# GpSimd's position tables ahead of its first two loads, in an attention and expert kernel whose loads all go through one queue

## The chip, the core and the metric

The kernel runs on one core of a Trainium2 chip. The core has five engines that run side by side, each with its own list of instructions: TensorE (PE, with its weight loads shown apart as PEld), VectorE (DVE), ScalarE (ACT), GpSimd (POOL) and SyncE (SP). Sixteen DMA engines move data between the device memory and the core. SP and POOL issue the transfers of this kernel: what SP issues is listed as hardware_dynamic (queue q1), what POOL issues as software_dynamic (queue q0). The metric is the device time of one execution in microseconds; lower is better.

## What is computed

Attention over 4 batches, 8 heads, 768 positions and 64 values a head, with a mask for each head, followed by a mixture of 8 experts with 4 slots each:

```python
scores = scale * np.matmul(q, k.transpose(0, 1, 3, 2))
pos = np.arange(S)
rel = pos[:, None] - pos[None, :]
causal = rel >= 0
stream_keep = causal & (is_sink | in_win)          # the first 4 keys, or the last 64
mask = np.where(retr, full_mask, stream_mask)      # by head
a = softmax(np.where(mask, scores, -1e9))
x = np.matmul(a, v)  # then reshaped to (3072, 512)
logits = x @ phi                                   # 32 slots
d = softmax of logits over the tokens
slot_input = d.T @ x
h = np.maximum(slot_input[e] @ w1[e], 0.0); slot_out[e] = h @ w2[e]   # e = 0..7
out = softmax of logits over the slots @ slot_out
```

The inputs are float32: q, k and v of 6.3 MB each and w1 and w2 of 16.8 MB each. POOL's loads convert to bfloat16 on the way.

## The kernel before

The kernel first makes a list of operations (`pl.op`), each with the engines that can run it, a priority, what it depends on and a function `emit` that writes its instructions. A planner (`Plan.run`, line 69) puts them in order by its own estimates of time; the functions are then called in that order (lines 1178 to 1185), and the order in which they are called is the order of the instructions on each engine. Within one `emit`, the instructions follow each other as they are written.

All loads but three are issued by POOL through the helper `dma` (line 343), which appends to a chain: each issue depends on the one before (`fifo[0]`), and from the ninth on also on the landing of the load eight places ahead (line 345). So POOL's issues have a fixed order: the first halves of q, k and v of batch 0 (`load_part`, line 361), their second halves, half of the first expert's w1, then tiles of the other batches with weights between them, and at the end the last w2 in halves (lines 976 to 979), which are put into memory that the attention has set free.

The three other loads are SP's (`sp_front`, line 480), issued without any wait: the other half of the first expert's w1 in float32 (1 MB, `w0f`), the head flags (`ri`) and phi (`phf`).

`tables` (line 412) is what the change moves: six small instructions on POOL.

```python
def tables(o):
    nc.gpsimd.iota(jrow, ...)          # 128x128, column numbers
    nc.gpsimd.iota(pc[:, 0:1], ...)    # 128x1, partition numbers
    nc.gpsimd.iota(tq, ...)            # 1x256
    nc.gpsimd.iota(krow, ...)          # 1x128
    nc.gpsimd.memset(unit, 1.0)        # 1x256
    nc.gpsimd.iota(pc_i[:, 0:1], ...)  # 128x1, integers
```

From the first two VectorE makes the identity (`head_const`, line 422), which ScalarE reorders for the first transposes (`ident_u`, line 500); from the others TensorE and VectorE make the distances between positions for the masks (`emit_td`, `key_pos`, lines 429 to 442) and the slots' tables (line 465). All of these operations depend on the operation `tables` (`o_tab`, line 488).

On POOL the order at the start is: issue of q's first half, issue of k's first half, `tables`, issue of v's first half, two memsets (`ones`), issues of the second halves. TensorE transposes the first half of q when it has landed and the reordered identity is there (`transposes`, line 599); until then it runs matmuls on zeros (`fill`, line 425). Phi is cast, transposed twice and spread in between (lines 548 to 555).

After the attention come the expert layers: each expert's w1 product and w2 product as its weights land (lines 1008 to 1084), then the product that makes the output (`out_tile`, line 1125) and the stores (`store`, line 1146), most of them from SP.

Of the kernel before, what the change touches and what calls it, by code (L numbers as in the profile page):

```python
# [226 lines left out]
def kernel(  # L227
# [81 lines left out]
    def tr_bf(s, n):  # L309
        return trb[s].bitcast(BF16)[:, 0:n]  # L310
# [10 lines left out]
    pl = Plan({"S8": 11, "QT": 2, "KT": 2, "VT": 1, "VB": 2, "VF": 3, "PT": 2, "PTX": 2, "XB": 2,  # L321
               "XT": 1, "SC": 2, "TR": 2, "PV": 1, "BK": 8})
# [6 lines left out]
    def on(eng, occ, late=0.18):  # L329
        return {eng: (occ, occ + late)}  # L330

    def copy(o, dst, src):
        if o.eng == "ACT":
            nc.scalar.copy(dst, src)  # L334
        else:
            nc.vector.tensor_copy(dst, src)  # L336
# [4 lines left out]
    fifo, chain = [None], []  # L341

    def dma(name, nbytes, buf, dst, src, deps=()):
        if len(chain) >= 8:
            deps = list(deps) + [chain[-8]]
        iss = pl.op("issue " + name, on("POOL", 0.645, 1.4), -100, deps=list(deps) + [fifo[0]],
                    acq=[buf] if buf else [], lead=1.3, emit=lambda o: nc.gpsimd.dma_start(dst(), src))  # L347
        fifo[0] = iss
        took = nbytes / (395000.0 if nbytes == 1 << 20 and name != "w0" else 423000.0)
        chain.append(pl.op("land " + name, {"DMA": (took, took + 1.85 + 0.05 * len(chain))}, -100, deps=[iss] + chain[-1:], lead=5.2))  # L350
        return chain[-1]

    def raw_view(buf, p0, p1):
        return slots[buf.slot][p0:p1, 0:8 * KB].rearrange("p (i x) -> p i x", i=2)

    def raw_src(x, b, n0, n1):
        a = srcs[x][b].rearrange("(i n) (t s) d -> n t i (s d)", i=2, s=32)[n0:n1]
        return a.rearrange("n t i x -> (n t) i x")


    def load_part(x, b, part=None):
        if part is None:
            raws[x, b] = buf = Buf("S8")
            lands[x, b] = dma(f"{x}{b}", 96 * 2 * 8192, buf, lambda: raw_view(buf, 0, 96), raw_src(x, b, 0, 4))
        else:
            if part == 0:
                raws[x, b] = Buf("S8")
            buf = raws[x, b]
            src = srcs[x][b].rearrange("(i n) (y s) d -> n y i (s d)", i=2, s=16)[2 * part:2 * part + 2]
            lands[x, b, part] = dma(f"{x}{b}.{part}", 96 * 2 * 4096, buf if part == 0 else None,  # L370
                                    lambda: half_view(buf, part), src.rearrange("n y i e -> (n y) i e"))

    def half_view(buf, part):
        return slots[buf.slot][0:96, 2048 * part:2048 * (part + 1)].rearrange("p (i x) -> p i x", i=2)
# [6 lines left out]
    def w_mem(i):  # L381

        m = late_mem[i]() if i in late_mem else slots[wbuf[i].slot][:, :]
        return m.rearrange("p (h x) -> p h x", h=2)[:, :, 0:4 * KB]
# [27 lines left out]
    def tables(o):  # L412
        nc.gpsimd.iota(jrow, [[1, 128]], base=0, channel_multiplier=0, allow_small_or_imprecise_dtypes=True)
        nc.gpsimd.iota(pc[:, 0:1], [[0, 1]], base=0, channel_multiplier=1, allow_small_or_imprecise_dtypes=True)
        nc.gpsimd.iota(tq, [[128, 2], [1, 32], [32, 4]], base=0, channel_multiplier=0,
                       allow_small_or_imprecise_dtypes=True)
        nc.gpsimd.iota(krow, [[-1, 32], [-32, 4]], base=0, channel_multiplier=0,
                       allow_small_or_imprecise_dtypes=True)
        nc.gpsimd.memset(unit, 1.0)
        nc.gpsimd.iota(pc_i[:, 0:1], [[0, 1]], base=0, channel_multiplier=1)  # L420
# [33 lines left out]
    def head_flags(o, n):  # L454
        cp = nc.scalar.copy if o.eng == "ACT" else nc.gpsimd.tensor_copy
        for a, j0, j1 in ((1, 1, 4), (0, 0, 1)):
            cp(fmx[:, n, :, j0:j1, :].rearrange("p i j d -> p i (j d)"),
               thr[:, a, n::4].rearrange("p (i o) -> p i o", o=1).to_broadcast([P, 2, 66 * (j1 - j0)]))
# [24 lines left out]
        nc.sync.dma_start(phf, moe_phi.rearrange("(p a) s -> p (a s)", a=4))  # L483

    load_part("q", 0, 0)
    load_part("k", 0, 0)
    o_sp = pl.op("front", on("SP", 2.0, 4.8), -100, emit=sp_front)
    fifo[0] = o_tab = pl.op("tables", on("POOL", 1.65, 0.0), -100, deps=[fifo[0]], emit=tables)
    load_part("v", 0, 0)
    def pone(o):  # L490
        for b_ in vbs:
# [33 lines left out]
    for n in range(4):  # L525
        o_fm[n] = pl.op(f"fm{n}", on("ACT", 0.65) if n == 0 else on("POOL", 0.9), -8 if n == 0 else T * n - 3.5,
                        deps=[o_fl], emit=lambda o, n=n: head_flags(o, n))
# [15 lines left out]
    def phi_t2(o):  # L543
        for n in range(4):
# [8 lines left out]
                  emit=lambda o: nc.vector.tensor_copy(  # L553
                      phi4, tr_bf(pb2.slot, 4 * NS).rearrange("p (n r s) -> p n r s", n=4, r=1).to_broadcast(
                          [P, 4, 4, NS])))
# [3 lines left out]
    def load_tile(ti):  # L559

        tbuf[ti], tland[ti], p0 = Buf("S8"), [], 0
        for x, b, x0, x1 in TILES[ti]:
# [8 lines left out]
                  emit=lambda o, x=x: nc.gpsimd.tensor_copy(w_mem(0)[:, 0, KB * x:KB * (x + 1)],  # L571
                                                            w0f[:, KB * x:KB * (x + 1)])) for x in range(4)]
# [82 lines left out]
    def evs(x, b, n):  # L655
        return ev[x, 0, n // 2] if b == 0 else [e for x0, x1, e in ev[x, b] if x0 < 6 * n + 6 and x1 > 6 * n]
# [15 lines left out]
    def mask_emit(b, n, g):  # L672
        def f(o):
            pT = pTs[PTb[b, n].slot]
            mh = msk[:, n::4, :]
            if g < 2:
                pT = pT[:, :, 1024 * g:1024 * (g + 1)].rearrange("p i (a c) -> p i a c", a=2)[:, :, :, 0:256]
                mh = mh[:, :, 256 * g:256 * g + 512].rearrange("p i (a c) -> p i a c", a=2)
            else:
                pT, mh = pT[:, :, 2048:2304], mh[:, :, 256:512]  # L680
            nc.vector.tensor_tensor(pT, pT, mh, op=ALU.mult)  # L681
        return f
# [6 lines left out]
    for b in range(B):  # L689
        for n in range(4):  # L690
# [5 lines left out]
            def emit_v2(o, n=n, tr=tr):  # L696
                t = tr_bf(tr.slot, 768)
                for j in range(6):
# [3 lines left out]
                      emit=emit_v2, mode="full", mm=6)  # L702
# [9 lines left out]
            def emit_vf(o, b=b, n=n, p=p):  # L712
# [4 lines left out]
                           emit=emit_vf)  # L717

            PTb[b, n] = Buf("PT")
            for kk, g in enumerate(range(5)):  # L720
# [19 lines left out]
                for m, gs in enumerate(MGROUPS):  # L740
                    if gs[-1] == g:
                        o_m = pl.op(f"MK.{p}.{m}", on("DVE", [0.605, 0.605, 0.335][m]), key + 0.3,
                                    deps=[expo[p, x] for x in gs] + [o_hm[n]], emit=mask_emit(b, n, m))
# [3 lines left out]
        for ns in ([(0, 1), (2, 3)] if b == 0 else [(0, 1, 2, 3)]):  # L747
            sc = Buf("SC")

            def emit_lx(o, b=b, sc=sc, ns=ns):  # L750
# [4 lines left out]
                      deps=list(dict.fromkeys(e for n in ns for x in "qk" for e in evs(x, b, n))),  # L755
# [10 lines left out]
            def emit_mx(o, b=b, ns=ns):  # L766
# [5 lines left out]
                      emit=emit_mx)  # L772
# [5 lines left out]
    for b in range(B):  # L778
        for n in range(4):
# [9 lines left out]
            for i in iorder:  # L789
                deps, need = [v2e[p], vfo[p]] + [o_z][p:], set()  # L790
# [7 lines left out]
                def emit_pv(o, b=b, n=n, p=p, i=i, pv_at=pv_at):  # L798
                    pT = pTs[PTb[b, n].slot]
                    vb = vbs[VBb[b].slot]  # L800
                    for h in range(2):
                        bk, c = pv_at(h, i)
                        for j in range(i + 1):
# [3 lines left out]
                            else:  # L807
# [5 lines left out]
                             deps=list(dict.fromkeys(deps)) + ([last] if last else []),  # L813
# [8 lines left out]
            for i0, i1 in halves:  # L822
                part = f"{p}" if i1 - i0 == 6 else f"{p}.{i0}"

                def emit_nm(o, i0=i0, i1=i1, b=b, n=n, p=p):
# [3 lines left out]
                    else:  # L829
# [8 lines left out]
                                 deps=[pvo[i1 - 1], XBb[b].op], acq=[XBb[b]] if n == 0 else [], rel=[PVb[p]],  # L838
                                 emit=emit_nm)
# [25 lines left out]
        if b < B - 1:  # L865
# [19 lines left out]
            def emit_tt(o, te=te):  # L885
                for i in range(6):
# [5 lines left out]
                           emit=lambda o, te=te: copy(o, elg.rearrange("p i s -> p (i s)"), tr_bf(te.slot, 6 * NS)))  # L892
# [8 lines left out]
        else:  # L901
# [3 lines left out]
            for i0 in (0, 3):  # L905
                a = pl.op(f"LG.{b}" if i0 else f"LGb.{b}", pe(25, 3), kb - 6.0, deps=[a, xhalf[i0]], rel=[XTb[b]],
                          emit=lambda o, lg=lg, f=emit_lg, i0=i0: f(o, lg, ns=(3,), i0=i0, i1=i0 + 3), mode="full", mm=3)
# [82 lines left out]
    def emit_si(o):  # L990
        t = trb[si.slot][:, 0:4 * NS].rearrange("p (a s) -> p a s", a=4)
        sv = slot_sc.rearrange("p (di do) -> p do di", do=4)
        for do in range(4):
# [4 lines left out]
                  emit=lambda o: nc.vector.tensor_copy(siT.rearrange("p a s -> p (a s)"), trb[si.slot][:, 0:4 * NS]))  # L998
# [110 lines left out]
    for c in range(2):  # L1109
        def emit_so(o, c=c):  # L1110
# [3 lines left out]
            else:  # L1114
# [3 lines left out]
                          emit=emit_so))  # L1118
# [103 lines left out]
```

## Time and profile before

| | us |
|---|---|
| median of 3 runs | 147.88 |
| lowest and highest | 147.87, 148.34 |
| the profiled execution | 147.56 |
| its span, first to last instruction | 145.8 |

The mean granted clock of TensorE over the span is 0.944 of the full one. How to read the rows that follow: in the timeline and the chain of waits the first number is the start in microseconds from the first instruction, the second the time taken, then engine, line and operation, what it writes and what it reads; in square brackets stands how long the engine sat idle before it and what ended the wait. SPq and POOLq are the two engines' own sequencers. A DMA instruction of POOL is shown while the descriptors are made, not while the data move. Landing is counted from the issue. In the table of DMA queues a row gives packets, megabytes written and the time of the packets as a share of sixteen engines; the share can exceed 100%, since packets of one engine overlap.

### The profile page before, as it was taken

The numbers are of one execution on the slowest core, as the hardware profiler recorded it, in microseconds if no ns is written. First come the engines' busy times: TensorE is split into PE (matmuls) and PEld (weight loads), VectorE is DVE, ScalarE is ACT, GpSimd is POOL, SyncE is SP. The second block draws the span as 40 slices with busy tenths as digits, with TensorE's granted clock in tenths as the row PEclk, the third lists the DMA queues.
The fourth block names the chain that finished last, engine by engine and source line by source line (L and its number), as shares of the span: only waits on it lengthen the run. The fifth ranks groups of instructions, "written<-read, shape, count | busy, mean of one in ns | idle before, by whom it ended". The sixth has DMA issues, their size and how long they took to land.

```text
span 145.8 us, 4941 instructions
## 1 busy us (share of the span) xinstructions
PE 124.6 (85%) x2134; PEld 82.3 (56%) x2134; DVE 110.8 (76%) x254; ACT 107.9 (74%) x147; POOL 40.5 (28%) x73
## 2 busy tenths in 40 slices
PE   6959989999999999999989999999959899869100
PEld 4437566676776758776548766666737355444000
DVE  1796399999999999999799899999983312449700
ACT  3152799999999988999998999999971461549300
POOL 6988631310311470100170011405380000110000
PEclk9985699999999999999999999999995999999965
DMA  5999999999999999999999999999999999999995
GB/s 135 277 208 211 215 215 214 212 216 214 215 214 214 216 215 214 216 214 211 215 214 215 214 216 219 212 217 215 217 210 215 211 194 197 185 321 362 407 420 247
DMA packets 14648, 33.40 MB, mean 229 GB/s; under 512 B 867, under 2 KB 7651, under 8 KB 14115
## 3 DMA queue, kind: packets, MB, share of 16 engines
q0 software_dynamic: 11184, 26.22, 92.9%
q1 hardware_dynamic: 3442, 6.88, 12.7%
q8 instruction: 16, 0.26, 0.6%
q14 instruction: 6, 0.04, 0.1%
HBM read 52.49 MB, written 6.29 MB: 403 GB/s over the span
## 4 chain that ended last, share of the span: by engine, by line
PE 28%; DVE 25%; DMA 18%; ACT 15%; issue 6%; POOL 1%; SPq 0%; DVEq 0%; ACTq 0%; POOLq 0%
DMA qk<-in_moe_w_dram 15%; ACT pt L735 11%; PE sc L665 6%; DVE pt L681 5%; PE pv L809 5%; DVE xv L833 5%; DMA phf<-in_moe_phi_dram 4%; DVE qk L336 3%; PE tr L613 3%; PE tr L639 3%; PE bk L1130 3%; PE tr L872 2%; DVE slot L1140 2%; DVE vf L714 2%; PE tr L845 2%
## 5 line engine op out<-in xcount | busy, mean ns | idle before, releaser
L735 ACT ACTIVATE pt<-sc 128x1024 bf16<-128x1024 f32 x80 | 77.0, 1049 | 3.0 <-PE sc L665 2.8
L665 PE MATMUL sc<-qk 64*128 64x512 bf16 (+3 forms) x256 | 31.3, 311 | 1.2 <-ACT pt L735 0.8
L681 DVE TENSOR_TENSOR pt<-pt,msk 128x1024 bf16<-128x1024 bf16 (+1 forms) x48 | 29.0, 609 | 2.0 <-ACT pt L735 1.8
L809 PEld LDWEIGHTS <-pt 128*128 128x128 bf16 x640 | 23.7, 98 | 6.2 <-issue 5.2
L809 PE MATMUL pv<-vx,pt 128*128 128x65 bf16 x320 | 25.9, 194 | 0.3 <-DVE xv L833 0.2
L809 PE MATMUL pv<-vf,pt 128*128 128x65 bf16 x320 | 21.6, 196 | 0.9 <-DVE xv L833 0.9
L347 POOL DMA_DIRECT2D slot<-in_moe_w_dram x11 | 7.8, 705 | 39.3 <-PE tr L639 29.5
L639 PE MATMUL tr<-ident,slot 128*64 128x128 bf16 (+1 forms) x448 | 16.3, 219 | 0.4 <-ACT qk L334 0.3
L336 DVE COPY qk<-tr 128x768 bf16<-128x768 bf16 (+2 forms) x33 | 15.1, 481 | 1.5 <-PE tr L613 1.3
L639 PEld LDWEIGHTS <-slot 128*64 128x64 bf16 (+1 forms) x448 | 13.1, 109 | 5.1 <-issue 4.8
L833 DVE TENSOR_TENSOR xv<-pv,rs 128x768 bf16<-128x768 f32 (+1 forms) x17 | 15.5, 910 | 0.6
L665 PEld LDWEIGHTS <-qk 64*128 64x128 bf16 x256 | 10.4, 94 | 9.6 <-issue 3.3
L1140 DVE TENSOR_SCALAR slot<-bk,rrow 128x256 f32<-128x256 f32 (+1 forms) x19 | 9.2, 561 | 2.2 <-PE bk L1130 2.2
L896 POOL COPY expT<-eT 128x192 bf16<-128x192 bf16 x12 | 7.4, 657 | 12.2 <-ACT eT L879 12.2
L336 DVE COPY xv<-tr 128x512 bf16<-128x512 bf16 (+2 forms) x20 | 7.9, 409 | 2.4 <-PE tr L613 2.2
L845 PE MATMUL tr<-ident,xv 128*128 128x128 bf16 x96 | 8.4, 224 | 1.3 <-DVE xv L833 0.9
L613 PE MATMUL tr<-ident_u,slot 96*64 96x96 bf16 x192 | 7.3, 238 | 1.9 <-DVE phi L553 1.4
L613 PEld LDWEIGHTS <-slot 96*64 96x64 bf16 x192 | 6.3, 133 | 4.5 <-issue 4.1
L336 DVE COPY xT<-tr 128x768 bf16<-128x768 bf16 (+1 forms) x14 | 7.5, 538 | 1.1 <-PE tr L845 1.1
L1138 ACT ACTIVATE slot<-bk,rrow 128x256 f32<-128x256 f32 (+1 forms) x17 | 7.7, 569 | 0.9 <-PE bk L1130 0.9
L699 PE MATMUL tr<-ident,xv 128*128 128x128 bf16 x96 | 8.1, 220 | 0.0
L845 PEld LDWEIGHTS <-xv 128*128 128x128 bf16 x96 | 6.0, 99 | 2.9 <-DVE xv L833 1.7
(123 smaller groups left out, 169.0 us busy)
## 6 DMA issues: line engine op xcount, KB each, us to landing
slot<-in_moe_w_dram POOLq DMA_DIRECT2D x10, 1024.0 KB, 24.5
out_dram<-slot SPq DMA_DIRECT2D x3, 1024.0 KB, 6.2
out_dram<-slot SPq DMA_DIRECT2D x10, 256.0 KB, 3.2
slot<-in_q_dram POOLq DMA_DIRECT2D x2, 768.0 KB, 19.4
slot<-in_k_dram POOLq DMA_DIRECT2D x2, 768.0 KB, 24.1
qk<-in_moe_w_dram SPq DMA_DIRECT2D x1, 1024.0 KB, 6.1
slot<-in_v_dram POOLq DMA_DIRECT2D x2, 512.0 KB, 21.3
qk<-in_moe_w_dram POOLq DMA_DIRECT2D x1, 1024.0 KB, 17.5
```

The lines of the kernel that those rows point to most:

```text
L336: nc.vector.tensor_copy(dst, src)
L347: acq=[buf] if buf else [], lead=1.3, emit=lambda o: nc.gpsimd.dma_start(dst(), src))
L613: nc.tensor.transpose(t[64 * i:64 * (i + 1), :, :, s, :], rv[:, i, 8 * c + s, :], ident_u)
L639: nc.tensor.transpose(t[64 * i:64 * (i + 1), :, s, :], rv[:, i, 8 * c + s, :], ident[0:R, 0:R])
L665: nc.tensor.matmul(scb[sc.slot][:, i, c:c + 128 * nb], kk, qq.rearrange("p b c -> p (b c)"), start=True, stop=True)
L681: nc.vector.tensor_tensor(pT, pT, mh, op=ALU.mult)
L699: nc.tensor.transpose(t[:, 128 * j:128 * (j + 1)], vT[:, 6 * n + j, :], ident)
L735: nc.scalar.activation(pTs[PTb[b, n].slot][:, :, 512 * g:512 * (g + 1)], scb[sc.slot], ACT.Exp, scale=scale)
L809: nc.tensor.matmul(pvb[:, bk, c:c + 65], lt, rhs, start=(j == 0), stop=(j == i))
L833: nc.vector.tensor_tensor(xo, pvw[:, :, :, 0:64], r.rearrange("p i (j o) -> p i j o", o=1).to_broadcast([P, 2, i1 - i0, 64]), op=ALU.mult)
L845: nc.tensor.transpose(t[:, 128 * i:128 * (i + 1)], xv[:, i, 128 * n:128 * (n + 1)], ident)
L1140: nc.vector.tensor_scalar(d, banks[bf.slot][:, 0:w], sc_, None, op0=ALU.mult)
```

## The change

The tables' six instructions are written ahead of the first load's issue, inside its `emit`; the operation `tables` stays in the list, in its place and with its estimate of time for the planner, and writes nothing any more. The planner's list, its estimates and its dependences are the same.

```diff
     load_part("q", 0, 0)
+    first = fifo[0].emit
+
+    def tables_first(o):
+        tables(o)
+        first(o)
+
+    fifo[0].emit = tables_first
     load_part("k", 0, 0)
     o_sp = pl.op("front", on("SP", 2.0, 4.8), -100, emit=sp_front)
-    fifo[0] = o_tab = pl.op("tables", on("POOL", 1.65, 0.0), -100, deps=[fifo[0]], emit=tables)
+    fifo[0] = o_tab = pl.op("tables", on("POOL", 1.65, 0.0), -100, deps=[fifo[0]])
     load_part("v", 0, 0)
```

On POOL the order at the start becomes: `tables`, issue of q's first half, issue of k's first half, issue of v's first half, `ones`, and so on as before.

## The prediction

> **What bounds the kernel now.** I read the page first, for the DMA row and the queues; then a table of stretches, for whether that row is the same everywhere; then the chain of waits at its end. Rows of the page:
>
> ```profile
> span 145.8 us, 4941 instructions
> PE 124.6 (85%) x2134; PEld 82.3 (56%) x2134; DVE 110.8 (76%) x254; ACT 107.9 (74%) x147; POOL 40.5 (28%) x73
> DMA  5999999999999999999999999999999999999995
> q0 software_dynamic: 11184, 26.22, 92.9%
> slot<-in_moe_w_dram POOLq DMA_DIRECT2D x10, 1024.0 KB, 24.5
> ```
>
> The table of stretches (start and end, length, then busy time of PE, its weight loads, DVE, ACT and POOL with instruction counts, granted clock, DMA share, GB/s):
>
> ```profile
> 6.00:40.00 34.00, 30.82 (x576) 21.08 (x575) 29.29 (x73) 26.87 (x35) 15.29 (x27) 0.90 1.08 213
> 40.00:74.00 34.00, 33.23 (x639) 23.19 (x636) 32.23 (x72) 32.30 (x43) 8.07 (x13) 1.00 1.06 214
> 74.00:108.00 34.00, 32.15 (x609) 22.58 (x606) 32.64 (x67) 32.72 (x40) 10.07 (x15) 1.00 1.06 214
> ```
>
> And the last long step of the chain, with what follows it:
>
> ```profile
> 108.08 21.34 DMA qk<-in_moe_w_dram
> 129.46 0.43 PE bk L1055 x8
> ```
>
> No compute engine is full over the span, while the DMA engines are at or above nine tenths in every slice but the first and the last. From 6 to 108 us the share is 1.06 to 1.08 and the rate 213 or 214 GB/s in all three stretches, although the work of the other engines changes: the queue that GpSimd fills (q0) never runs dry. A weight load lands 24.5 us after its issue, and a megabyte at 214 GB/s takes 4.9 us, so some five loads always stand in line. A compute engine or an issue that comes a microsecond late is therefore paid out of this backlog. The end is different: the last weight half lands at 129.4 us, matmuls start on it at 129.46, and the remaining 16.3 us hang on it. So the question is one alone: when does this stream start, and does the change move that start?
>
> **The start, which the change touches.** The timeline of the first microseconds:
>
> ```profile
> 0.73 0.38 SPq L481 DMA_DIRECT2D qk<-in_moe_w_dram  x1
> 0.85 0.24 DVE L505 MEMSET zt<- 128x224 uint32 x1 [0.85 <-PEq L1203]
> 1.33 0.78 POOL L347 DMA_DIRECT2D slot<-in_q_dram  x1 [0.89 <-POOLq L1203]
> 2.11 0.65 POOL L347 DMA_DIRECT2D slot<-in_k_dram  x1
> 2.83 0.29 POOL L413 IOTA xT<- 128x128 f32 x1
> 3.23 0.63 DVE L423 TENSOR_SCALAR ident<-xT,pc 128x128 bf16<-128x128 f32 x1 [2.14 <-POOL pc L414]
> 4.35 0.12 POOL L420 IOTA pc_i<- 128x1 int32 x1
> 4.42 0.67 POOL L347 DMA_DIRECT2D slot<-in_v_dram  x1
> 7.14 0.40 DVE L548 CAST phi<-phf 128x128 bf16<-128x128 f32 x1 [0.23 <-DMA phf<-in_moe_phi_dram]
> 8.85 0.53 PE L613 MATMUL tr<-ident_u,slot 96*64 96x96 bf16 x16
> ```
>
> What the DMA engines did then, in short windows (queue, packets, megabytes, share of 16 engines). In order: 0 to 4.8 us, 2.1 to 4.2, 4.2 to 4.8 (with its rate), 4.8 to 5.1, 4.8 to 5.4, 5.4 to 6.0 and 6.0 to 7.2 (with its rate); the last row is the load issued at 1.33 us, with its time to landing.
>
> ```profile
> q1 hardware_dynamic: 119, 0.93, 62.3%
> ...
> q1 hardware_dynamic: 70, 0.57, 82.0%
> ...
> DMA packets 35, 0.25 MB, mean 411 GB/s; under 512 B 3, under 2 KB 5, under 8 KB 5
> ...
> q0 software_dynamic: 1, 0.00, 3.6%
> ...
> q0 software_dynamic: 13, 0.03, 24.8%
> ...
> q0 software_dynamic: 48, 0.10, 91.9%
> ...
> DMA packets 129, 0.25 MB, mean 208 GB/s; under 512 B 7, under 2 KB 7, under 8 KB 129
> ...
> slot<-in_q_dram POOLq DMA_DIRECT2D x1, 384.0 KB, 7.4
> ```
>
> Until 4.8 us only SP's queue (q1) moves data: half of the first expert's weights, at 0.93 MB by then. The first packet of GpSimd's queue comes just before 5.1 us, 3.77 us after the issue at 1.33. From 6.0 us it runs alone at 208 GB/s. By 6.0 it had moved 0.03 MB up to 5.4 and 0.10 MB after, which is 0.6 us at that rate; it stands where a queue would that had started at 5.4 at its full rate. The first q half lands at 1.33 + 7.4 = 8.73 us, and TensorE transposes it from 8.85.
>
> **The change, part by part.** Nothing is added or removed; five iotas and a memset change places with the issues of the first q and the first k half.
>
> *The tables come earlier.* They run from 2.83 until the next issue starts at 4.42: 1.59 us. The other engines leave the start at 0.73 (SP) and 0.85 (DVE), so on GpSimd they would run from about 0.8 to 2.39. VectorE waited 2.14 us for them and would build the identity some 2 us earlier. That is worth nothing: the next thing on VectorE that matters waits for phi, which lands by 7.1 us, and TensorE's first transposes wait for q at 8.73. The work that hides the gain is these two transfers; without them it would be up to 2 us.
>
> *The two issues come later.* Before its first issue GpSimd idles until 1.33, some 0.5 us longer than the others. If that is preparation for a DMA, it can lie under the tables, as for v, whose issue at 4.42 starts while the iota from 4.35 to 4.47 still runs. Then q is issued at 2.39, a delay of 1.06 us. If it is GpSimd's own start, everything shifts by the tables: q at 2.92, a delay of 1.59. I take 1.06, since the row of v shows no gap, and keep 1.59 for the range. The k half keeps its distance behind q and is delayed as much; it is not missed, since the q half ahead of it occupies the stream for 0.384 MB / 0.208 = 1.8 us.
>
> *The issues behind.* With 0.78 + 0.65 us for q and k, v would be issued at 3.82 instead of 4.42, and all that follows up to 0.6 us earlier, or, with the late start, at the old time. Each of them joins a line that is already there, so neither costs nor gains anything. SP's queue is passed by nothing: its three issues depend on no table.
>
> *What the delay costs.* If the 3.77 us from issue to first packet goes along with the issue, the first packet comes at 5.1 + 1.06 = 6.16 us. SP's transfers are over by 6.0, so it then runs at full rate at once, and the loss is 6.16 − 5.4 = 0.76 us. With the other start it is 5.1 + 1.59 − 5.4 = 1.29 us. Below, the bound is nothing (first rival) or a gain (second rival). What is late next: q's landing, the first transposes and all of the compute behind, which has its 24.5 us of backlog; and each load of the stream by the same 0.76 us, to the last one at 129.4.
>
> *Sum.* The profiled execution took 147.56 us, 1.76 outside its span of 145.8. With 0.76 it is 148.32. The runs have a median of 147.88, 0.32 above that execution, so on their footing I expect 147.88 + 0.76, about 148.6 us; the forecast's own range is 148.3 to 149.2.
>
> A rule to weigh. No packet of q0 moved before 4.8 us though q had been issued at 1.33. The Trainium skill, "DMA: Bandwidth & Descriptors", section "Queues, rings and completion order", says that each DMA engine takes turns between the queues that have work, packet by packet; by that rule q0 would have mixed with SP's packets if it had been ready, so it was not ready, and the delay counts in full, as in the sum. The same page, "Latency and other measured facts", gives about 1 us to the first byte for a transfer issued from GpSimd; by that figure q was ready at some 2.3 us and only stood in line, and the sum would be zero. The trace as it stands agrees with one of the two at most.
>
> **Rivals.**
>
> *First: q stands in line behind SP's megabyte, and a later issue only stands there for less time.* For it: near the end, where GpSimd issues a store, the whole of issue, transfer and landing takes 3.0 us:
>
> ```profile
> 126.78 1.44 POOL L1149 DMA_DIRECT2D out_dram<-slot  x2 [17.83 <-DVE slot L1140]
> ...
> out_dram<-slot POOLq DMA_DIRECT2D x1, 128.0 KB, 3.0
> ```
>
> That is less than the 3.77 us to q's first packet, and the stream was busy there. Also, GpSimd's first packet comes just as SP's queue runs out. Against it: from 2.1 to 4.2 us SP's packets filled 82% of the engines' time, so a packet that was ready would have found room. If it holds, a q issued at 2.39 is ready by 2.39 + 3.0 = 5.4 at the latest, so the loss is between 0 and 0.3 us: 147.9 us (147.7 to 148.2).
>
> *Second, on the other side: the issues themselves slow SP's megabyte, and moving them sets it free.* Place: 2.1 to 4.2 us, right behind the first issue and beside the second. There 0.57 MB took 2.1 us, 273 GB/s, against 411 GB/s from 4.2 to 4.8. At 411 the same bytes take 1.39 us; SP's queue would be through 0.7 us sooner and GpSimd's could begin at 5.4 − 0.7 = 4.7. It decides if a q issued at 2.39 is ready by then, 2.3 us after its issue, and if the megabyte does not meet the moved issues instead. Price: up to 0.7 us gained, 147.2 us, with half of it 147.5. Against it stands the row of 1.5 to 2.1 us:
>
> ```profile
> DMA packets 14, 0.11 MB, mean 191 GB/s; under 512 B 0, under 2 KB 0, under 8 KB 0
> ```
>
> Before the second issue, SP's queue was slower still (0.11 MB, 191 GB/s), which looks like a start-up of its own.
>
> **How the numbers follow.** Forecast (the delay reaches the stream, by 0.76 to 1.29 us, 0.4 at least): 0.58. First rival: 0.24. Second rival: 0.18. A measurement of this kernel tells 0.3%, 0.44 us, from no change; its runs lie 147.87 to 148.34. The forecast lies beyond that on the slow side, the first rival within it, and of the second most lies beyond it on the fast side: faster 0.16, same 0.26, slower 0.58. The range goes from 147.3, which leaves out the larger gains of the second rival, to 149.4, just above the late start of GpSimd (147.88 + 1.29 = 149.2).
>
> **What would show it.** In the changed profile: the tables from about 0.8 us and the q issue near 2.4 (near 2.9 means the larger delay); the first q0 packet at 6.2 us with idle DMA engines ahead of it, or still at 5.1 (first rival), or at 4.7 with SP's queue gone sooner (second); q landing at 9.5 us instead of 8.73; an identity built by 2 us with nothing gained behind; the stretches from 6 to 108 us still at 213 or 214 GB/s; and the last weight half landing at 130.2 instead of 129.4. The forecast is wrong if q0's first packet does not move, or if the stream starts late and the last landing does not follow, which would mean that the line is not what sets the end.

## The result, and the profile after

The changed kernel takes 148.38 us (median), the kernel before 147.71 on the same chip: a ratio of 1.0047 with a 95% interval from 1.0032 to 1.0063, or 0.7 us more. One of the 22 runs of the changed kernel, at 553.66 us, was in the slow state and does not count in the ratio. The prediction was 148.6 us, from a loss of 0.76. The size came out; the way to it did not, as the rows show.

The page of the changed kernel:

```profile
span 146.5 us, 4941 instructions
PE 122.4 (84%) x2134; PEld 81.1 (55%) x2134; DVE 111.2 (76%) x254; ACT 108.5 (74%) x147; POOL 40.7 (28%) x73
DMA  5999999999999999999999999999999999999995
q0 software_dynamic: 11184, 26.22, 92.6%
```

The same three stretches of it (start and end, length, busy time of PE, PEld, DVE, ACT and POOL, granted clock, DMA share, GB/s):

```profile
6.00:40.00 34.00, 29.55 (x586) 20.29 (x586) 29.57 (x73) 28.10 (x36) 14.81 (x26) 0.95 1.08 212
40.00:74.00 34.00, 33.42 (x641) 23.23 (x639) 32.18 (x71) 32.19 (x43) 9.01 (x15) 1.00 1.06 214
74.00:108.00 34.00, 31.43 (x593) 22.06 (x591) 32.62 (x68) 32.30 (x39) 10.08 (x14) 1.00 1.06 214
```

The span grew from 145.8 to 146.5 us. No stage of the middle is slower, except that the first stretch moves 212 GB/s where it moved 213. The last long step of the chain, and below it the first matmuls behind it, from the timeline of TensorE:

```profile
107.18 22.93 DMA qk<-in_moe_w_dram
```

```profile
130.15 0.40 PE L1062 MATMUL bk<-qk,xT 128*32 128x256 bf16 x8 [1.51 <-DMA qk<-in_moe_w_dram]
```

The last weight half was issued 0.9 us earlier than before (107.18 for 108.08), so the compute was not late. (In a second profile of each kernel, below, the two issues come at 108.23 and 108.20, so that lead is not a fixed effect of the change.) It landed 0.7 us later, at 107.18 + 22.93 = 130.11 us for 129.42. The tail behind it is 146.5 − 130.11 = 16.4 us for 145.8 − 129.4 = 16.4 before: the whole difference is in that landing.

The start of the changed kernel, in its timeline:

```profile
0.84 0.24 POOL L413 IOTA xT<- 128x128 f32 x1 [0.39 <-POOLq L1210]
1.20 0.67 DVE L423 TENSOR_SCALAR ident<-xT,pc 128x128 bf16<-128x128 f32 x1
2.43 0.79 POOL L347 DMA_DIRECT2D slot<-in_q_dram  x1
3.22 0.65 POOL L347 DMA_DIRECT2D slot<-in_k_dram  x1
3.85 0.64 POOL L347 DMA_DIRECT2D slot<-in_v_dram  x1
6.78 0.48 DVE L555 CAST phi<-phf 128x128 bf16<-128x128 f32 x1 [0.60 <-DMA phf<-in_moe_phi_dram]
8.60 0.53 PE L620 MATMUL tr<-ident_u,slot 96*64 96x96 bf16 x16
```

And what its DMA engines did, in the windows 0 to 4.8 us, 4.8 to 5.1, 4.8 to 5.4, 5.4 to 6.0, 6.0 to 7.2 and 8 to 14 (queue, packets, megabytes, share of 16 engines); the last row is q's first half, with its time from issue to landing:

```profile
q1 hardware_dynamic: 124, 0.94, 61.4%
...
q0 software_dynamic: 3, 0.01, 12.5%
...
q0 software_dynamic: 18, 0.04, 38.7%
...
q0 software_dynamic: 40, 0.08, 87.8%
...
q0 software_dynamic: 123, 0.24, 110.6%
...
DMA packets 647, 1.22 MB, mean 204 GB/s; under 512 B 50, under 2 KB 50, under 8 KB 647
...
slot<-in_q_dram POOLq DMA_DIRECT2D x1, 384.0 KB, 6.1
```

The kernel before, in its window from 8 to 14 us:

```profile
DMA packets 659, 1.25 MB, mean 208 GB/s; under 512 B 49, under 2 KB 49, under 8 KB 659
```

q is issued 1.1 us later, and its first packets still come before 5.1 us: three by then, where there was one, and 18 by 5.4 us, where there were 13. But then the stream is slower for a while: 40 packets for 48 from 5.4 to 6.0, 123 for 129 up to 7.2, 647 for 659 from 8 to 14 us. That makes some 20 packets of 2 KB too few by 14 us (917 for 937), 41 KB, or 0.2 us at 208 GB/s. In the second profiles it is 30 (933 for 963). The kernel before differs by 26 between its own two profiles, so this step is small beside its spread; both profiles of the changed kernel lie below both of the kernel before. By 108 us q0 is still 0.04 and 0.07 MB behind in the two pairs, 0.2 and 0.3 us at 208 GB/s.

The landing shows the rest. The trace has 16 landing events for each load, which are read here as one from each of the 16 DMA engines; for the last weight half, with the kernels of the first set of experiments:

```
last weight half, parts landing (us)   first    median   last
kernel before                          126.69   128.41   129.42
changed kernel                         126.65   128.52   130.11
kernel before, once more               126.42   128.15   129.17
changed kernel, once more              126.71   128.30   129.98
twin tables                            127.33   129.24   130.13
tables between q and k                 126.48   128.34   129.44
```

In the changed kernel the median part is 0.1 to 0.15 us late at the end. The last one is 0.7 to 0.8 us late, and the matmuls wait for the last one. The parts no longer end so close together: 3.5 and 3.3 us from first to last, where it was 2.7.

### The profile page after: what moved, and what is told of

The parts are those of the page before. It is cut to its first block, busy times and chain, and to the rows that moved or that the text cites. A ratio compares the mean times of both kernels' runs of the same rounds, so it can differ in the third digit from the quotient of the medians.

```text
span 146.5 us, 4941 instructions
## 1 busy us (share of the span) xinstructions
PE 122.4 (84%) x2134; PEld 81.1 (55%) x2134; DVE 111.2 (76%) x254; ACT 108.5 (74%) x147; POOL 40.7 (28%) x73
## 4 chain that ended last, share of the span: by engine, by line
PE 34%; DVE 28%; DMA 19%; ACT 6%; issue 5%; POOL 1%; SPq 0%; DVEq 0%; ACTq 0%; POOLq 0%
DMA qk<-in_moe_w_dram 16%; PE sc L672 8%; PE pv L816 7%; DVE pt L688 6%; DVE xv L840 5%; ACT pt L742 4%; PE tr L646 4%; DMA phf<-in_moe_phi_dram 4%; DVE qk L336 3%; PE bk L1137 3%; PE tr L620 3%; DVE xv L336 3%; PE tr L852 2%; DVE vf L721 2%; DVE vx L336 2%
## 5 line engine op out<-in xcount | busy, mean ns | idle before, releaser
L852 PE MATMUL tr<-ident,xv 128*128 128x128 bf16 x96 | 8.1, 219 | 1.5 <-DVE xv L840 0.9
L620 PEld LDWEIGHTS <-slot 96*64 96x64 bf16 x192 | 5.6, 119 | 4.8 <-issue 4.1
L1137 PE MATMUL bk<-msk,expT 128*128 128x256 bf16 (+1 forms) x36 | 7.5, 364 | 0.8 <-ACT msk L1120 0.8
L620 PE MATMUL tr<-ident_u,slot 96*64 96x96 bf16 x192 | 6.4, 220 | 2.1 <-DVE phi L560 1.0
L721 DVE TENSOR_TENSOR vf<-vx,fmx 128x528 bf16<-128x528 bf16 x16 | 7.9, 495 | 0.3
```

The lines of the kernel that those rows point to most:

```text
L620: nc.tensor.transpose(t[64 * i:64 * (i + 1), :, :, s, :], rv[:, i, 8 * c + s, :], ident_u)
L721: nc.vector.tensor_tensor(vfs[VFb[p].slot], vv, fmx[:, n], op=ALU.mult)
L852: nc.tensor.transpose(t[:, 128 * i:128 * (i + 1)], xv[:, i, 128 * n:128 * (n + 1)], ident)
L1137: nc.tensor.matmul(banks[bf.slot][:, 0:w], out_lhs(gi, r), slot_out[:, cs], start=True, stop=True)
```

## The experiments

**First set: which of the moves costs it?** Four kernels on one chip, where the kernel before took 147.53 us.

*Twin tables.* Six instructions like the tables', writing to memory not yet in use, ahead of q's issue; the real tables stay behind k's issue. It delays the loads, without giving anyone the tables early.

```diff
+    def twin_first(o):
+        nc.gpsimd.iota(slot_acc[:, 0:128], [[1, 128]], channel_multiplier=0, **kw)
...
+        first(o)
+    fifo[0].emit = twin_first
```

> A twin of the six table instructions, writing to scratch, stands ahead of q's issue; the real tables stay behind k's issue. So q is issued at 2.4 us and k at 3.2 as in the changed kernel, but the tables and v come later than in either (v near 5.5). Late issue (q and k 1.1 us later cost the time, whatever stands ahead of them): 1.003 to 1.008 times the kernel before, with GpSimd's first packet still near 5.0 us. Early tables (the cost comes from their users, or from the issues behind k, coming 0.6 to 2 us earlier): 1.000, within 0.002. My prediction's step (the wait from issue to first packet moves along): first packet at 6.2 us.

148.53 us, ratio 1.007 (1.0042 to 1.0098). Its timeline, and below it its window from 6.0 to 7.2 us:

```profile
2.44 0.79 POOL L347 DMA_DIRECT2D slot<-in_q_dram  x1
3.22 0.65 POOL L347 DMA_DIRECT2D slot<-in_k_dram  x1
3.87 0.28 POOL L413 IOTA xT<- 128x128 f32 x1
```

```profile
DMA packets 109, 0.21 MB, mean 176 GB/s; under 512 B 6, under 2 KB 6, under 8 KB 109
```

The loss is there, although nothing got its tables early, so the early tables are not needed for it: the late issues are enough. But it takes another form here. The slow stretch is deeper (176 GB/s, and 868 packets by 14 us), and at the end all parts of the last weight half are 0.9 to 1.1 us later than in the kernel before on this chip, with no wider spread (2.8 us). Why the stream starts more slowly than in the changed kernel, with q and k issued at the same times, is open; the twin also makes v and the loads behind it 1.1 us later than in the kernel before.

*Tables between q and k.* Only k is late.

```diff
+    def tables_second(o):
+        tables(o)
+        second(o)
+    fifo[0].emit = tables_second      # the issue of k's first half
```

> The tables stand between q's issue (1.33 us, as before) and k's (near 3.8). Late issue of q alone as the cause: 1.000, within 0.002. If it is the second issue, or the early tables, that costs: 1.003 to 1.006. v is issued at the same 4.4 us as before.

147.87 us, ratio 1.0017 (0.9997 to 1.0038). Its timeline, and below it its window from 6.0 to 7.2 us:

```profile
1.33 0.78 POOL L347 DMA_DIRECT2D slot<-in_q_dram  x1 [0.89 <-POOLq L1210]
2.20 0.28 POOL L413 IOTA xT<- 128x128 f32 x1
3.79 0.68 POOL L347 DMA_DIRECT2D slot<-in_k_dram  x1
```

```profile
DMA packets 132, 0.25 MB, mean 208 GB/s; under 512 B 10, under 2 KB 10, under 8 KB 132
```

k came 1.7 us late, and the stream kept its 208 GB/s. So it is mainly q's issue that counts, the first of the queue; the interval reaches to 1.0038, so a small cost of the late k is not excluded.

*The two kernels once more*, unchanged, for their profiles and for the spread between chips.

> The changed kernel once more, for its ratio on this chip and a second profile. If the 0.47% comes from which DMA engine starts last and is hit by the 16 KB instruction loads, the last weight half lands 0.4 to 0.9 us later than in the kernel before while the first of its 16 parts lands at the same time within 0.15 us. If the whole stream starts later, all 16 parts land later by about the same.

> The kernel before, unchanged: ratio 1.000 within 0.0015, which shows what these rounds can tell, and a second profile of it. If the spread of the DMA engines at the start is the kernel's own and not chance, the five late engines of the first q half (0.7 to 1.06 us behind the median) are there again and the last weight half has 2.6 to 2.9 us between its first and last part.

The changed kernel 148.63 us, 1.007 (1.0048 to 1.0091); the kernel before 147.65 us, 0.9999 (0.9977 to 1.0022). The loss is repeated; their landings stand in the table above. The last part is 0.8 us later, as the spread alone would have it, but the first one is 0.3 us later too, more than the 0.15 allowed for. So it is some of both forms: the stream a little behind, the slowest part more so.

**Second set: what does q's queue do when nothing lies ahead of it?** SP's megabyte was held back in both kernels, by a small VectorE copy into its memory that waits for the position columns; VectorE's work grows by that copy. The flags and phi, 66 KB, stay where they were and are over by 2.8 us.

```diff
     def key_pos(o):
...
+        nc.vector.tensor_copy(w0f[:, 0:1], pc[:, 2:3])
+        nc.sync.dma_start(w0f, moe_w1[0].rearrange(...)[0])
...
     def sp_front(o):
-        nc.sync.dma_start(w0f, moe_w1[0].rearrange(...)[0])
```

> The kernel before, with SP's megabyte (half of the first expert's w1) issued only once VectorE has made the key positions, at some 5 us or later, so that it no longer lies ahead of q. Theory 'cover' (q stands in line behind SP's megabyte; a transfer of GpSimd's needs at most 2.5 us from issue to first packet): q, issued at 1.33, has its first packet at 3.9 us or sooner and lands at 7.0 to 7.5. Theory 'fixed wait' (3.6 to 3.8 us from issue to first packet, as the prediction had it): first packet still at 5.0 to 5.1. The time by itself is some 148 to 149.5 us by either, since the megabyte now competes with the stream.

> The changed kernel with SP's megabyte held in the same way. Cover: with nothing to hide it the whole delay of q's issue, 1.1 us, reaches its first packet (at 4.9, beside 3.9 in the run before) and the time is 0.8 to 1.2 us above that of the run before. Fixed wait: first packet at 6.1, the time also some 1.1 above. If the difference of the two kernels has nothing to do with when q's data begin to flow, it stays at about 0.7 us.

With the old order 148.86 us, 1.0081 (1.0063 to 1.01); with the tables first 149.85 us, 1.0136 (1.0117 to 1.0155): 1.0 us apart, nearly the whole delay of the issue. All parts of the last weight half shift with it: the first, median and last by 1.0, 0.9 and 1.3 us. The held megabyte is issued at 6.00 and 5.48 us, so the two kernels also differ in which loads it passes. The windows of the old order, from 2.5 to 4.0 us and from 4.2 to 5.2:

```profile
q0 software_dynamic: 27, 0.06, 54.1%
...
DMA packets 106, 0.22 MB, mean 217 GB/s; under 512 B 0, under 2 KB 0, under 8 KB 106
```

With the tables first, from 2.5 to 4.0 us, 4.2 to 5.2 and 5.3 to 6.3:

```profile
q0 software_dynamic: 8, 0.02, 26.7%
...
DMA packets 31, 0.06 MB, mean 63 GB/s; under 512 B 0, under 2 KB 0, under 8 KB 31
...
DMA packets 99, 0.20 MB, mean 203 GB/s; under 512 B 0, under 2 KB 0, under 8 KB 99
```

In the first kernel q is issued at 1.32 us, its first packet starts at 2.83, sooner than the 3.9 expected, and the queue is at its full rate from 4.2 us on; in the second these are 2.43, 3.92 and 5.3. (The starts of first packets are read from the trace.) So the first packet comes 1.5 us after the issue and the full rate 2.9 us after it, in both. That is the queue's slow start; and the 1.5 us are less than half of the 3.77 in the kernel before, so most of that wait came with the megabyte. Carried over to the two kernels of the change, as an estimate, the slow start would be over at 1.33 + 2.9 = 4.2 us in the kernel before, while SP's megabyte still ran. In the changed kernel it would reach to 2.43 + 2.9 = 5.3 us, past the first free engines at 4.9 (q's first packet there starts at 4.94).

**Third set: half a megabyte more in front, twice.** A longer line should hide the late issue altogether. First on SP's queue, behind phi:

```diff
     def sp_front(o):
...
+        nc.sync.dma_start(pt_mem[:, 0:2048].bitcast(F32), moe_w1[1].rearrange(...)[0][:, 0:1024])
```

> The kernel before, with another half megabyte on SP's queue behind phi (a part of w1 again, into memory that is written anew later), so that SP's line ends at some 6.2 us instead of 5.0. Cover: q's first packet at 6.2, all loads and the time some 1.2 us later than in the kernel before, about 148.8.

> The changed kernel with the same half megabyte more. Cover with a lead (the late issue costs because q's descriptors have less time before the line is free): q, issued at 2.43, now has the 3.8 us that it had in the kernel before; first packets as quick as in the run before, and the time equal to it (-0.3 to +0.3 us). If it is another effect of the late issue (which DMA engine the later work meets, places of later issues), the time stays some 0.7 us above the run before.

149.87 us, 1.0144 (1.0126 to 1.0162), and 150.95 us, 1.0215 (1.0195 to 1.0234): 1.1 us apart, where equal times were expected, and the first 1.1 us above its expected 148.8. The window from 6.0 to 7.5 us, of the old order and then of the tables first:

```profile
q0 software_dynamic: 73, 0.15, 54.8%
q1 hardware_dynamic: 60, 0.24, 47.8%
```

```profile
q1 hardware_dynamic: 72, 0.27, 66.2%
q0 software_dynamic: 23, 0.05, 28.0%
```

This pair did not make the line that was meant. SP issues the half megabyte at 1.93 us, behind q's issue in one kernel (1.33) and ahead of it in the other (2.43). In the first, q shares the engines with it, some 73 packets to 60; in the second q mostly stands behind it, 23 to 72, and all engines together move less, 0.32 MB for 0.39. The pair changes the order of the queues as well, so it says nothing on the lead. Why the second moves less in total is open.

Then from ScalarE's queue at the very start, ahead of q's issue in both kernels:

```diff
     def sp_front(o):
+        nc.scalar.dma_start(pt_mem[:, 0:2048].bitcast(F32), moe_w1[1].rearrange(...)[0][:, 0:1024])
```

> The kernel before, with another half megabyte (a part of w1, into memory that is written anew later) issued by ScalarE at the very start, ahead of q's issue in time in both kernels of this pair, so that the line ahead of q lasts some 1.2 us longer. By the theory of a slow start (a transfer of GpSimd's needs some 2.7 us from its issue to its full rate; the kernel before hides that behind SP's megabyte, the changed one not quite): q's packets flow from some 6.0 us, the time is some 1.2 us above the kernel before, about 148.9.

> The changed kernel with the same half megabyte. Slow start: q, issued at 2.43, is at its full rate by 5.2, well ahead of the end of the line; q's first half lands as in the run before, and the time is equal to it (-0.3 to +0.3 us). If the loss has another cause that goes with the late issue, whatever lies ahead of q, the time is 0.7 to 1.1 us above the run before, as in the pair with the half megabyte behind phi.

With the old order 150.29 us, 1.0189 (1.0176 to 1.0203); with the tables first 150.01 us, 1.0173 (1.0159 to 1.0188): equal, within 0.3 us. q's first half, with its time from issue to landing, in the one and in the other:

```profile
slot<-in_q_dram POOLq DMA_DIRECT2D x1, 384.0 KB, 8.8
```

```profile
slot<-in_q_dram POOLq DMA_DIRECT2D x1, 384.0 KB, 7.6
```

Issued at 1.33 and 2.42, q lands at 10.1 and at 10.0 us. With a longer line ahead of both issues the late one costs nothing in the median time. In the two profiles the last weight half still spreads wider in the second (3.4 us for 2.8) and its last part lands at 131.69 us for 131.28, so the longer line does not remove the spread. Both kernels are 1.1 to 1.4 us slower than expected, and the reason is open. The change from one line to the other is slow in both, but half a microsecond at 153 GB/s instead of 208 loses only 0.13 us; and the stretch behind the last landing is 17.1 and 16.8 us, where it was 16.4. The window from 7.0 to 7.5 us of the old order, then of the tables first:

```profile
DMA packets 77, 0.08 MB, mean 153 GB/s; under 512 B 25, under 2 KB 46, under 8 KB 77
```

```profile
DMA packets 72, 0.08 MB, mean 162 GB/s; under 512 B 10, under 2 KB 40, under 8 KB 72
```

**Two more on the same chip.** The tables behind three issues, as a possible gain:

```diff
+    early = [fifo[0].emit]            # v's issue
+    fifo[0].emit = None
+    def loads_first(o):
+        for f in early:
+            f(o)
+        tables(o)
+    o_tab.emit = loads_first
```

> The other way round: the tables behind the issues of q, k and v (q 1.33, k 2.11, v 2.7, tables 3.4 to 5.0). By the prediction and by the slow start alike nothing changes, since only q's issue counts: q lands as in the kernel before, the time within -0.3 and +0.3 us of it. If every issue ahead of the tables helps, it is up to 0.5 us faster than the kernel before.

147.72 us, 1.0017 (1.0002 to 1.0031). As in the kernel before, q lands 7.4 us after an issue at 1.33. An issue of v 1.7 us earlier is worth nothing, and no version of this study beats the kernel before.

The changed kernel with an early read of q's rows:

```diff
     def tables_first(o):
+        nc.scalar.dma_start(touch, q_src[:, :, 0:16])
         tables(o)
         first(o)
...
+    touch = sb.tile([96, 2, 16], F32, name="touch")
```

> The changed kernel, with a small transfer of ScalarE's ahead of everything that reads 64 bytes of each row of q's first half. If the slow first packets of GpSimd's queue are first reads of this memory, they are quick now and the time falls by 0.3 to 0.7 us to that of the kernel before. If they come from how the queue starts (its descriptors), they stay and the time stays some 0.7 us above the kernel before, or a little more for the added transfer.

148.88 us, 1.0099 (1.0076 to 1.0121). Inconclusive: the small transfer itself landed 5.8 us after its issue at 0.74, at 6.5 us, when q's packets already ran (from 5.24 us).

```profile
touch<-in_q_dram ACTq DMA_DIRECT2D x1, 12.0 KB, 5.8
```

## Why the prediction was right in size and wrong in its way

*What bounds the kernel*: right. The stream sets the end, the stretches kept their rates, the tail its 16.4 us, and compute that was 0.9 us ahead at the last issue in this profile gained nothing.

*The tables come earlier and bring nothing*: right. They ran from 0.84 to 2.43 us, the identity began 2.0 us earlier, and the cast of phi and the first transposes still waited for their transfers, to 6.78 and 8.60 us.

*The two issues come later*: right. q was issued at 2.43 (2.39 predicted), k at 3.22, v at 3.85 (3.82 predicted). What GpSimd does ahead of its first issue lay under the tables. That a late k and an early v count for little is shown by the tables between q and k, and by the tables behind v.

*What the delay costs*: the step that failed is "If the 3.77 us from issue to first packet goes along with the issue, the first packet comes at 5.1 + 1.06 = 6.16 us." It came at 4.94 us. The 3.77 us were not q's own: 1.5 us are, as the held megabyte showed (1.32 to 2.83 and 2.43 to 3.92 us), and the rest was standing in line. With it fell "q landing at 9.5 us": it landed at 2.43 + 6.1 = 8.5, no later than the 8.73 of the kernel before. "SP's transfers are over by 6.0, so it then runs at full rate at once" failed too: the queue started sooner and ran below its rate for a while. By the prediction's own test, "The forecast is wrong if q0's first packet does not move", its mechanism is refuted. That the sum of 0.76 us was nearly met is luck: the 0.7 us were made up of something else.

*What stands in its place.* In the held pair GpSimd's queue needed 2.9 us from its first issue to its full rate, and other work ahead can hide that. With the megabyte gone, q's delay of 1.1 us cost 1.0 us; with half a megabyte more in place ahead of both issues it cost nothing. This much is shown. With SP's megabyte, which sets engines free from 4.9 us on, the slow start reaches by this estimate 0.4 us into the free time, and the profiles have the stream 0.2 to 0.3 us behind.

The rest of the 0.7 us is in the spread of the 16 landings, and only observed: the slowest part lands 0.7 to 0.8 us late in the two profiles of the changed kernel beside the two of the kernel before, the median one 0.1 to 0.15. One row bears on where it comes from. The window from 14.2 to 16.0 us of the changed kernel has one load of instructions:

```profile
q8 instruction: 1, 0.02, 3.3%
```

That is 0.033 × 16 × 1.8 us = 0.95 us for one packet of 16 KB, and there are sixteen such loads in a run. The parts of k's second half, which land about then, lie 2.1 us apart in the changed kernel and 1.2 before, while those of q's second half, just ahead, lie 1.3 and 1.2 apart. The second profiles have the same step, from 1.1 to 1.9 us in the changed kernel and none in the kernel before. It looks as if the first such load met an engine that was already among the last, but no run here moves it to another engine, so this is argued and not shown. It is also not enough by itself: with the tables between q and k the parts step from 1.0 to 1.8 us at the same place, and the last weight half still lands at 129.44 us. And the twin loses its time with the spread at 2.8 us. Where this part of the loss comes from stays open.

*The rivals.* The first, q standing in line behind SP's megabyte, had the mechanism. Its price of 0 to 0.3 us fits the stream and the median part, but the time follows the slowest one, which the prediction did not look at. What it held against the rival, "a packet that was ready would have found room", was wrong: with the megabyte held back q's packets flowed at 2.83 us, and with it ahead the same issue's came at 5.09. The second rival brought no gain: SP's queue had moved 0.94 MB by 4.8 us, for 0.93 before. The issues were not gone from beside it, since those of q, k and v now stood there from 2.43 to 4.5 us; but ahead of that, from 1.5 to 2.4 us with no issue of GpSimd's, SP's queue moved only 164 GB/s, for 146 in the kernel before with the issues of q and k beside it. So it is slow there without the issues too.

The rule that was weighed was applied too finely. The Trainium skill, "DMA: Bandwidth & Descriptors", section "Queues, rings and completion order", lets an engine change queues only when it has drained a packet of some 9 to 17 descriptors. What the profile counts as packets are taken here for smaller pieces: SP's megabyte is 1 MB / 8 KB = 128 of them, 8 for each engine, fewer than one packet of the rule. By that reading q waits for all 8 though it is ready, and this trace agrees: q's first packet starts at 5.09 us, as the megabyte ends. No run here shows where a packet of the rule ends, so the reading itself is not shown. The same page's 1 us to the first byte ("Latency and other measured facts") is short here: 1.5 us were measured, and 2.9 to the full rate.

## What to carry to other kernels

When a queue's first packet comes long after its first issue, look at what the DMA engines do meanwhile: if another queue ends just then, the gap may be a line. Take the line away and measure: here 1.5 of 3.77 us were left, and the queue's own start is what decides how late its issue may come. Put small work behind the first issue of the queue that feeds the kernel; in this kernel it need not go further, since a later issue that joined a standing line cost little or nothing (k 1.7 us later, 1.0017). And where the end hangs on one transfer, look at the landing of its last part: here it was 0.7 to 0.8 us late with the median part 0.1 to 0.15.

## What was not expected

In one pair two queues shared the DMA engines or stood one behind the other, depending on which was issued first: 73 packets to 60 in 1.5 us with q issued ahead of SP's half megabyte, 23 to 72 with it behind, and then the engines together moved 0.32 MB for 0.39. At the change from SP's pieces to GpSimd's the rate dropped to 153 and 162 GB/s for half a microsecond, where GpSimd's queue alone moved 203 to 217; more than half of the packets in those windows are under 2 KB, so small pieces may be the reason, which is not settled. And the one packet of a single instruction load took 0.95 us.
